# A long-convolution layer and two dense layers in one kernel: the filter's first layer on two 64-row tiles, signal factors in one transfer, one weight rounding a unit later

## The chip, the cores and the metric

The kernel runs on one core of a Trainium2 chip. The metric is the device time of one execution in microseconds (us), as the median of three runs. One further execution was taken with the profiler; its trace is what is read below.

## The reference

Three steps follow each other on 12480 positions (S) of 128 channels (D). The first is a causal convolution of length S with a filter that a small network makes from 64 position features; the filter is damped by a window exp(-0.01 pos). The other two are dense layers of width 2048 with different gates.

```python
h_filt = (np.maximum(pos_emb @ w1, 0.0) @ w2) * np.exp(-0.01 * pos)[:, None]     # (S, 128); w1 is 64x64
u = x * v
y = np.fft.irfft(np.fft.rfft(u, n=2*S, axis=1) * np.fft.rfft(h_filt, n=2*S, axis=0)[None], n=2*S, axis=1)[:, :S]
a = x * y
h = a @ w_in;   a = (h * np.clip(h + 3, 0, 6) / 6) @ w_out                        # 128 -> 2048 -> 128
h = a @ w_in2;  a = np.where(h > 0, h, np.exp(np.minimum(h, 0)) - 1) @ w_out2
```

## The kernel before

**The convolution as matmuls.** Position p is written as 128·row + column, with 98 rows (`H1`) and 128 columns (`N2`). Every sequence is folded first: columns 64+i and 63-i are added and subtracted, so that there are 64 pairs i (`HN`) with two halves. The transforms along rows and columns are then matmuls with tables of cosines and sines (`t1`, `rows`, `gm`, `cs`, `ti`).

**The start, which the change touches.**

- Six matmuls on zeros (L184, the pool `warm`) come first on TensorE.
- The position features lie in HBM already folded and transposed: `posT` has the 64 features of one column of a pair on partitions 0 to 63 and those of the other on 64 to 127, and for each pair i a block of `H1` columns. SyncE loads it in eight pieces (L239), pieces 0 to 7 of 4, 6, 7, 8, 9, 10, 10, 10 pairs.
- `filter_hidden` (L345) runs over the 64 pairs in ten groups, `HIDDEN`: 4, 4, six times 8, 4, 4. For each pair one matmul (L349) multiplies 98 rows by a block-diagonal `w1` of 128 columns, so both halves come out of one pass over all 128 partitions. Each group has its own PSUM buffer `pr`, four of which exist.
- ScalarE takes the ReLU of the second half of each pair, scaled by `RATIO[i]`, into `au` (L357). VectorE then makes sum and difference with the ReLU of the first half (L370), 256 elements at a time, in one sweep for every four pairs; in the last two groups VectorE also takes over part of ScalarE's work (L363). The result is `Rf` (read as `Rp` here), in `qb`.
- `signal(n)` (L333) makes u = x·v for four channels (L338) and folds it (L340, L341). There are 32 such signals. For n = 0 and 1 it runs on GpSimd, from n = 2 on VectorE; each loads its x and v by two transfers (L315, L316) six signals ahead.
- `first` (L391) is the first transform: 8 matmuls of 180 columns, two halves onto different output partitions, and copies by ScalarE (L399). `first_u(n)` needs `signal(n)`; `first_r(c)` needs all of `Rf`. The order on TensorE is the layer, `first_u(0)`, `first_u(1)`, `first_r(0)`, `first_r(1)`, then two signals and one filter chunk in turn, 48 in all.

All order is written by hand: each engine runs its instructions in the order of the code, and all loads of this part stand in SyncE's queue. Eight transfers at most are under way on that queue: a ninth waits until the first has landed.

Later stages follow on TensorE: `second_r`, `second_h`, `second_u` (L448, L457, L467), the column transforms (L495, L531) and the inverse (L654).

**The dense layers.** A unit is a tile of 512 positions by 256 of the 2048 columns. On TensorE unit n has `mm1` (L841, into `h`) and, four units later, `mm2` (L885, into `o`). Between them ScalarE takes the activation (`act1`, L851), VectorE the gate (L862), ScalarE rounds the result to its upper part (`hi`, L870, into `gs`) and VectorE subtracts for the lower part (`lo`, L875). Weights are split in the same manner, in 16 quarters `w{i}_{q}` (matrix i, quarter q): loaded (L709), rounded on ScalarE (L781), and the lower half made on GpSimd in two pieces (L788). The table `pieces` says in which unit each of the two pieces of a quarter is made; the rounding comes one unit before the first. Each piece on GpSimd also waits for the newest instruction on VectorE in the program's order (`last_dve`).

Of the kernel before, what the change touches and what calls it, by code (L numbers as in the profile page):

```python
# [15 lines left out]
ALU = mybir.AluOpType  # L16
# [10 lines left out]
HN = N2 // 2  # L27
NM = HN + 1
SP = H1 * N2
HP = H1 * HN  # L30
HD = D // 2
SHIFT = H1 // 4
TT = 512
# [34 lines left out]
def tables():  # L68
    n1, k1, k2 = np.arange(H1), np.arange(NK), np.arange(N2)
    i, m, a = np.arange(HN), np.arange(NM), np.arange(H1) - 2 * SHIFT - 1  # L70
    w = 2 * np.pi * (np.outer(n1 - SHIFT, k1) % N1) / N1
    c, s = np.cos(w), np.sin(w)

    t1 = np.stack([np.stack([c, -s], axis=2), np.stack([-s, -c], axis=2)], axis=1)
    k = k1[:, None] + N1 * k2
    w = np.pi * (((2 * i + 1)[:, None, None] * k) % (2 * L)) / L
    gm = np.concatenate([np.cos(w), np.sin(w)], axis=0)

    w = 2 * np.pi * (np.outer(k2, m) % N2) / N2
# [45 lines left out]
    ratio = np.tile(np.repeat(RATIO, 2), (H1, 1))  # L125
    return [np.ascontiguousarray(z, dtype=np.float32) for z in (t1, gm, cs, ti, rows, column, ratio)]


def folded(z):

    z = np.pad(z, ((0, SP - S), (0, 0))).reshape(H1, N2, -1)
    return np.stack([z[:, HN:], z[:, HN - 1::-1]], axis=1).transpose(0, 3, 1, 2)


@with_exitstack
def tile_kernel(ctx, tc, xc, vc, xT, posT, w1_d, w2_d, moe_w, t1_d, gm_d, cs_d, ti_d, rows_d, column_d, ratio_d, outT):
    nc = tc.nc
    w_dram = [nc.dram_tensor(f"w_scratch{i}", (128, FF), F32, kind="Internal").ap() for i in range(4)]

# [82 lines left out]
    xts, vts, uts = uvs[:DEEP], uvs[DEEP:2 * DEEP], uvs[2 * DEEP:]  # L222
# [8 lines left out]
    Rf = qb[:H1, RW:RW + RF].rearrange("p (g s i t) -> p s i g t", s=2, i=HN, t=2)
    Rp = qb[:H1, RW:RW + RF].rearrange("p (g s x) -> p s g x", s=2, x=2 * HN)
    w1s = qb[:, HP:HP + 2 * FO]
    ratio = qb[:H1, HP + 2 * FO:HP + 2 * FO + N2]
    GI = 4
    nc.scalar.dma_start(w1s, w1_d)
    edges = [0, 4, 10, 17, 25, 34, 44, 54, 64]
    for a, b in zip(edges, edges[1:]):
        nc.sync.dma_start(pos_t[:, a * H1:b * H1], posT[:, a * H1:b * H1])  # L239
    tab = const.tile([128, 8 * NK], F32, name="tab")  # L240
    t1, rows = (tab[:H1, i * 4 * NK:(i + 1) * 4 * NK].rearrange("p (f k) -> p f k", f=2) for i in range(2))
# [103 lines left out]
    def filter_hidden(i0, n):  # L345
        pr = bank("pr", [128, 2, 2, FO // 2, GI, 2])
        t = au[:H1, i0 * FO:(i0 + n) * FO].rearrange("p (b g j t) -> p b g j t", g=FO // 2, j=GI, t=2)
# [5 lines left out]
        def relu(b):  # L353
            i = i0 + b * GI
            own = GI if i < HN - 2 * GI else 2
            for j in range(own):
                nc.scalar.activation(t[:, b, :, j], pr[:H1, b, 1, :, j], AF.Relu, scale=float(RATIO[i + j]))  # L357
            return own

        def folds(b, own):  # L360
            i = i0 + b * GI
            if own < GI:
                nc.vector.scalar_tensor_tensor(  # L363
                    t[:, b, :, own:].rearrange("p g j t -> p g (j t)"),
                    pr[:H1, b, 1, :, own:].rearrange("p g j t -> p g (j t)"), 0.0,
                    ratio[:, 2 * (i + own):2 * (i + GI)].unsqueeze(1).to_broadcast([H1, FO // 2, 2 * (GI - own)]),
                    op0=ALU.max, op1=ALU.mult,
                )
            for x, op in enumerate((ALU.add, ALU.subtract)):
                nc.vector.scalar_tensor_tensor(  # L370
                    Rp[:, x, :, 2 * i:2 * (i + GI)], pr[:H1, b, 0].rearrange("p g j t -> p g (j t)"), 0.0,
                    t[:, b].rearrange("p g j t -> p g (j t)"), op0=ALU.max, op1=op,
                )

        owns = [relu(b) for b in range(n // GI)]
        for b, own in enumerate(owns):
            folds(b, own)

    for n in range(DEEP):
        load_signal(n)  # L380
        if n == 0:
            nc.sync.dma_start(ratio, ratio_d)
            nc.sync.dma_start(t1.rearrange("p f k -> p (f k)"), t1_d)
        if n == 1:
            nc.sync.dma_start(rows.rearrange("p f k -> p (f k)"), rows_d)
            nc.sync.dma_start(column, column_d)
# [337 lines left out]
    for i, banks in enumerate(BATCHES):  # L724
# [243 lines left out]
```

## Time and profile before

| | |
|---|---|
| median of 3 runs | 1324.15 us (1323.83 to 1326.51) |
| profiled execution | 1326.66 us |
| its span, first to last instruction | 1324.8 us |
| TensorE busy | 1314.0 us, 99% of the span |
| VectorE busy | 1134.2 us, 86% |
| ScalarE busy | 1005.8 us, 76% |
| GpSimd busy | 411.0 us, 31% |

The span is the time between the program's first and last instruction; 1.9 us of the profiled execution lie around it. A busy engine is not one at its peak: matmuls overlap in the pipeline, and their rate has to be read from how many start in a stretch. In the rows PE is TensorE, PEld its weight loads, DVE VectorE, ACT ScalarE, POOL GpSimd and SP SyncE.

### The profile page before, as it was taken

The numbers are of one execution on the slowest core, as the hardware profiler recorded it, in microseconds if no ns is written. First come the engines' busy times: TensorE is split into PE (matmuls) and PEld (weight loads), VectorE is DVE, ScalarE is ACT, GpSimd is POOL, SyncE is SP. The second block draws the span as 40 slices with busy tenths as digits, with TensorE's granted clock in tenths as the row PEclk, the third lists the DMA queues.
The fourth block names the chain that finished last, engine by engine and source line by source line (L and its number), as shares of the span: only waits on it lengthen the run. The fifth ranks groups of instructions, "written<-read, shape, count | busy, mean of one in ns | idle before, by whom it ended". The sixth has DMA issues, their size and how long they took to land.

```text
span 1324.8 us, 23014 instructions
## 1 busy us (share of the span) xinstructions
PE 1314.0 (99%) x9184; PEld 1128.0 (85%) x9184; DVE 1134.2 (86%) x1209; ACT 1005.8 (76%) x1210; POOL 411.0 (31%) x319
## 2 busy tenths in 40 slices
PE   9999999999999999999999999999999999999998
PEld 9999998788888888888888888888888888888898
DVE  6769876699988888888888888888888888888897
ACT  5677663398878887788877887888778878887776
POOL 1027741334233322222223323222222223322223
PEclk9999999999999999999999999999999999999999
DMA  8945338610000000000000000000000000000000
GB/s 270 249 141 161 111 97 260 197 54 19 9 9 1 9 8 8 1 9 9 9 9 0 8 9 8 0 9 8 8 1 9 8 8 1 8 8 9 8 7 14
DMA packets 33676, 58.80 MB, mean 44 GB/s; under 512 B 3962, under 2 KB 10272, under 8 KB 33568
## 3 DMA queue, kind: packets, MB, share of 16 engines
q1 hardware_dynamic: 27232, 50.18, 12.5%
q10 hardware_dynamic: 6336, 7.15, 1.7%
q8 instruction: 72, 1.18, 0.4%
q14 instruction: 36, 0.29, 0.1%
HBM read 46.73 MB, written 10.58 MB: 43 GB/s over the span
## 4 chain that ended last, share of the span: by engine, by line
PE 96%; DVE 1%; ACT 1%; issue 1%; DMA 0%; POOL 0%; ACTq 0%; SPq 0%; POOLq 0%
PE o L885 39%; PE h L841 39%; PE pa L395 4%; PE y L654 3%; PE z L467 3%; PE q L495 2%; PE r L448 1%; PE h L457 1%; PE pr L349 1%; PE q L531 1%; DVE gs L875 0%; DMA w<-w_scratch 0%; DVE g L864 0%; ACT gs L870 0%; ACT qb L460 0%
## 5 line engine op out<-in xcount | busy, mean ns | idle before, releaser
L885 PE MATMUL o<-gs,w 128*128 128x512 f32 (+1 forms) x2400 | 566.2, 384 | 1.2 <-DVE gs L875 1.1
L885 PEld LDWEIGHTS o<-gs,w 128*128 128x128 f32 x2400 | 445.1, 188 | 87.4 <-DVE gs L875 1.7
L854 POOL TENSOR_SCALAR a<-a 128x1024 f32<-128x1024 f32 (+1 forms) x200 | 295.3, 1477 | 707.2 <-ACT a L853 705.9
L875 DVE TENSOR_TENSOR gs<-g,gs 128x1024 fp32r<-128x1024 f32 (+1 forms) x400 | 481.3, 1203 | 6.8 <-ACT gs L870 6.0
L870 ACT CAST gs<-g 128x1024 fp32r<-128x1024 f32 (+1 forms) x400 | 409.9, 1025 | 52.8 <-DVE g L862 51.4
L862 DVE SCALAR_TENSOR_TENSOR g<-a,h 128x1024 f32<-128x1024 f32 (+1 forms) x200 | 238.8, 1194 | 117.5 <-ACT a L851 117.2
L841 PE MATMUL h<-x,w 128*128 128x512 f32 (+1 forms) x1200 | 298.1, 384 | 0.2 <-DVE g L864 0.2
L841 PE MATMUL h<-xs,w 128*128 128x512 f32 (+1 forms) x1200 | 297.9, 384 | 0.0
L853 ACT ACTIVATE a<-h 128x1024 f32<-128x1024 f32 (+1 forms) x200 | 201.2, 1006 | 89.7 <-PE h L841 88.5
L841 PEld LDWEIGHTS h<-xs,w 128*128 128x128 f32 x1200 | 223.1, 188 | 44.6 <-DVE g L862 0.4
L841 PEld LDWEIGHTS h<-x,w 128*128 128x128 f32 x1200 | 223.0, 188 | 43.8 <-ACT gs L870 0.5
L851 ACT ACTIVATE a<-h,bounds 128x1024 f32<-128x1024 f32 (+1 forms) x200 | 218.9, 1094 | 49.7 <-PE h L841 49.5
L864 DVE SCALAR_TENSOR_TENSOR g<-a,h 128x1024 f32<-128x1024 f32 (+1 forms) x200 | 237.5, 1188 | 0.2 <-POOL a L854 0.2
L289 POOL TENSOR_TENSOR cv<-cv 128x256 int32<-128x256 int32 x32 | 23.4, 730 | 126.1 <-DVE cv L286 120.3
L395 PE MATMUL pa<-tab,qb 98*64 98x180 f32 x512 | 41.6, 316 | 0.1
L395 PEld LDWEIGHTS pa<-tab,qb 98*64 98x64 f32 x512 | 37.7, 138 | 2.7 <-ACT qb L399 0.4
L788 POOL TENSOR_TENSOR w<-w 128x256 fp32r<-128x256 f32 x26 | 19.2, 741 | 40.0 <-DVE gs L875 19.4
L271 ACT ACTIVATE cv<-cv 128x256 int32<-128x256 uint32 x32 | 14.2, 444 | 21.4 <-DMA cv<-in_mw 9.6
L654 PE MATMUL y<-qb 128*64 128x98 f32 (+3 forms) x688 | 25.5, 249 | 2.8 <-issue 2.8
L486 POOL TENSOR_TENSOR qb<-qb,bp 128x1024 f32<-128x1024 f32 (+1 forms) x12 | 27.0, 2247 | 3.9 <-DVE bp L481 3.9
L817 ACT COPY y<-o 128x512 f32<-128x512 f32 (+1 forms) x25 | 14.4, 578 | 17.5 <-PE o L885 17.5
L654 PEld LDWEIGHTS y<-qb 128*64 128x64 f32 (+1 forms) x688 | 23.1, 137 | 4.9 <-issue 3.6
(98 smaller groups left out, 880.4 us busy)
## 6 DMA issues: line engine op xcount, KB each, us to landing
uv<-in_xc SPq DMA_DIRECT2D x32, 196.0 KB
out_T<-y SPq DMA_DIRECT2D x23, 256.0 KB
qb<-in_gm SPq DMA_DIRECT2D x22, 256.0 KB
cv<-in_mw SPq DMA_DIRECT2D x21, 256.0 KB
au<-in_xT SPq DMA_DIRECT2D x16, 268.0 KB
w_scratch<-cv ACTq DMA_DIRECT2D x32, 128.0 KB
w<-w_scratch SPq DMA_DIRECT2D x16, 256.0 KB
cv<-in_vc SPq DMA_DIRECT2D x20, 196.0 KB
```

The lines of the kernel that those rows point to most:

```text
L395: nc.tensor.matmul(pa[f * HN:(f + 1) * HN, j, :2 * NK], lhsT=src(j, f), rhs=table[:, f], start=True, stop=True)
L467: nc.tensor.matmul(z[:, j], lhsT=gm_of(k0 + j), rhs=spectrum(hf, k0 + j, 1)[:, :, 0], start=True, stop=True)
L654: nc.tensor.matmul(y[c * HD:(c + 1) * HD, b, off:off + w], lhsT=lhsT, rhs=rhs[:, H1 - w:], start=(b, c) in fresh, stop=done, skip_group_ch ...
L841: nc.tensor.matmul(h[:, j], lhsT=wslice(2 * m - 2, a, 2 * u + j), rhs=x[:, b], start=i == 0, stop=i == 2)
L851: paced[0] = nc.scalar.activation(a, h, AF.Relu, bias=three)
L853: nc.scalar.activation(a, h, AF.Exp)
L854: nc.gpsimd.tensor_scalar(a, a, 1.0, 0.0, op0=ALU.min, op1=ALU.max)
L862: last_dve[0] = nc.vector.scalar_tensor_tensor(g, a, 6.0, h, op0=ALU.min, op1=ALU.mult)
L864: last_dve[0] = nc.vector.scalar_tensor_tensor(g, a, -1.0, h, op0=ALU.add, op1=ALU.max)
L870: nc.scalar.copy(t[:, 0], g)
L875: last_dve[0] = nc.vector.tensor_tensor(out=t[:, 1], in0=g, in1=t[:, 0].bitcast(F32), op=ALU.subtract)
L885: nc.tensor.matmul(o[:, :WID[t]], lhsT=wslice(2 * m - 1, a, 2 * u + j), rhs=gs[:, b, j], start=u == 0 and j == 0 and i == 0, stop=u == NU ...
```

## The change

- The window is zero from position 10398 (`ZERO`) on, so the filter has only 82 rows (`HR`) that count; the layer, its folds, `posT` and the table `rows` are cut to 82 rows.
- The layer's matmul per pair becomes two, each over 64 partitions and 64 columns of `w1`, written into the two PSUM banks of `pr`.
- The folds run over the whole group, 512 elements for 8 pairs, and VectorE no longer takes over ReLU work; the table `ratio` and its load are gone.
- x and v of a signal come in one transfer of 4 KB for each partition. The table `t1` comes before the first signal. Signals 0 and 2 run on GpSimd, 1 and 3 on VectorE.
- In the dense layers the two lower pieces of quarter `w0_3` are made in units 3 and 4 and not 2 and 3, so its rounding moves from unit 1 to unit 2.

```diff
+HR = -(-ZERO // N2)
-HP = H1 * HN
+HP = HR * HN
...
+    xvs = [
+        z[:H1, i * 2 * VT:(i + 1) * 2 * VT].rearrange("p (t d f i) -> p t d f i", t=2, f=2, i=HN)
+        for z, i in ((uv, 0), (uv, 1), (cv, 0), (cv, 1), (uv, 2), (uv, 3))
+    ]
...
-            c = slice(n * DC, (n + 1) * DC)
-            nc.sync.dma_start(xts[n % DEEP], xc[:, c])
-            nc.sync.dma_start(vts[n % DEEP], vc[:, c])
+            nc.sync.dma_start(xvs[n % DEEP], xv[:, n])
...
-    EARLY, LOOK = 2, 4
+    EARLY, LOOK = (0, 2), 4
...
-        e = nc.gpsimd if n < EARLY else nc.vector
+        e = nc.gpsimd if n in EARLY else nc.vector
...
     def filter_hidden(i0, n):
-        pr = bank("pr", [128, 2, 2, FO // 2, GI, 2])
+        pr = bank("pr", [128, 2, FO // 2, 8, 2])[:HR, :, :, :n]
...
         for j in range(n):
-            nc.tensor.matmul(
-                pr[:H1, j // GI, :, :, j % GI], lhsT=pos_t[:, (i0 + j) * H1:(i0 + j + 1) * H1],
-                rhs=w1s.rearrange("p (s g t) -> p s g t", s=2, t=2), start=True, stop=True,
-            )
...
+            for r in range(2):
+                p = slice(r * FO, (r + 1) * FO)
+                nc.tensor.matmul(
+                    pr[:, r, :, j], lhsT=pos_t[p, (i0 + j) * HR:(i0 + j + 1) * HR],
+                    rhs=w1s[p].rearrange("p (g t) -> p g t", t=2), start=True, stop=True,
+                )
+        for j in range(n):
+            nc.scalar.activation(t[:, :, j], pr[:, 1, :, j], AF.Relu, scale=float(RATIO[i0 + j]))
+        a, b = (z.rearrange("p g j t -> p g (j t)") for z in (pr[:, 0], t))
+        for x, op in enumerate((ALU.add, ALU.subtract)):
+            nc.vector.scalar_tensor_tensor(Rp[:, x, :, 2 * i0:2 * (i0 + n)], a, 0.0, b, op0=ALU.max, op1=op)
...
+    load_table(0)
+    load_signal(0)
+    load_signal(1)
+    load_table(1)
+    nc.sync.dma_start(column, column_d)
+    for n in range(2, DEEP):
         load_signal(n)
...
-        (1, 0): (1, 1), (0, 3): (2, 3), (1, 1): (4, 5), (1, 2): (6, 7), (1, 3): (8, 9), (2, 0): (10, 11),
+        (1, 0): (1, 1), (0, 3): (3, 4), (1, 1): (4, 5), (1, 2): (6, 7), (1, 3): (8, 9), (2, 0): (10, 11),
...
-        "xc": folded(x),
-        "vc": folded(v),
+        "xv": np.stack([folded(z).reshape(H1, D // 4, 4, 2, HN) for z in (x, v)], axis=2),
...
-        "posT": folded(inputs["pos_emb"]).transpose(2, 1, 3, 0).reshape(2 * FO, HP),
-        "w1": w1,
+        "posT": folded(inputs["pos_emb"], HR).transpose(2, 1, 3, 0).reshape(2 * FO, HP),
+        "w1": np.tile(inputs["w1"], (2, 1)),
```

On VectorE the program begins with two memsets; these rows stand behind them. Before:

```order
L370 SCALAR_TENSOR_TENSOR qb<-pr,au 98x32x8 x28
L363 SCALAR_TENSOR_TENSOR au<-pr,qb 98x32x4
L370 SCALAR_TENSOR_TENSOR qb<-pr,au 98x32x8 x2
L363 SCALAR_TENSOR_TENSOR au<-pr,qb 98x32x4
L370 SCALAR_TENSOR_TENSOR qb<-pr,au 98x32x8 x2
L338 TENSOR_TENSOR uv<-uv,cv 98x512
L340 TENSOR_TENSOR qb<-uv 98x4x64
L341 TENSOR_TENSOR qb<-uv 98x4x64
```

The same place on VectorE in the changed kernel:

```order
L357 SCALAR_TENSOR_TENSOR qb<-pr,au 82x32x8 x4
L357 SCALAR_TENSOR_TENSOR qb<-pr,au 82x32x16 x12
L357 SCALAR_TENSOR_TENSOR qb<-pr,au 82x32x8 x4
L336 TENSOR_TENSOR uv<-uv 98x512
L338 TENSOR_TENSOR cv<-uv 98x4x64
L339 TENSOR_TENSOR cv<-uv 98x4x64
```

32 folds and two ReLU pieces have become 20 folds, and the first signal behind them is number 1, which `first_u(1)` waits for; before it was number 2.

On SyncE this is the beginning of the queue of loads. Before:

```order
L239 DMA qb<-in_posT 128x392
L239 DMA qb<-in_posT 128x588
L239 DMA qb<-in_posT 128x686
L239 DMA qb<-in_posT 128x784
L239 DMA qb<-in_posT 128x882
L239 DMA qb<-in_posT 128x980 x3
L315 DMA uv<-in_xc 98x512
L316 DMA uv<-in_vc 98x512
L382 DMA qb<-in_ratio 98x128
L383 DMA tab<-in_t 98x360
L315 DMA uv<-in_xc 98x512
L316 DMA uv<-in_vc 98x512
```

The same place in the changed kernel:

```order
L360 DMA qb<-in_posT 128x328
L360 DMA qb<-in_posT 128x492
L360 DMA qb<-in_posT 128x574
L360 DMA qb<-in_posT 128x656
L360 DMA qb<-in_posT 128x738
L360 DMA qb<-in_posT 128x820 x3
L363 DMA tab<-in_t 98x360
L314 DMA uv<-in_xv 98x1024 x2
L363 DMA tab<-in_rows 98x360
L372 DMA column<-in_column 128x3
```

The pieces of `posT` stand first in both and are smaller; `ratio` is gone, and `t1` stands ahead of the first signal.

On ScalarE this is the start of the dense layers. The rounded weights are `w_0_...` for `w1_0`, `w_3_...` for `w0_3` and `w_1_...` for `w1_1`; `a<-h` is `act1`, `gs<-g` is `hi`. Before:

```order
L851 ACTIVATE a<-h,bounds 128x1024 x2
L781 CAST w_0_3439<-w_0_3439 128x512
L781 CAST w_3_3441<-w_3_3441 128x512
L870 CAST gs<-g 128x1024
L851 ACTIVATE a<-h,bounds 128x1024
L870 CAST gs<-g 128x1024
L851 ACTIVATE a<-h,bounds 128x1024
L870 CAST gs<-g 128x1024
L781 CAST w_1_3443<-w_1_3443 128x512
```

The same place in the changed kernel:

```order
L839 ACTIVATE a<-h,bounds 128x1024 x2
L769 CAST w_0_3460<-w_0_3460 128x512
L858 CAST gs<-g 128x1024
L839 ACTIVATE a<-h,bounds 128x1024
L858 CAST gs<-g 128x1024
L769 CAST w_3_3462<-w_3_3462 128x512
L839 ACTIVATE a<-h,bounds 128x1024
L858 CAST gs<-g 128x1024
L769 CAST w_1_3464<-w_1_3464 128x512
```

The rounding of `w0_3` has moved behind the `hi` of units 0 and 1. GpSimd's pieces keep their order.

## Rows read from the trace of the kernel before

**Rows 1.** The page: span, and the chain that ended last by engine.

```profile
span 1324.8 us, 23014 instructions
...
PE 96%; DVE 1%; ACT 1%; issue 1%; DMA 0%; POOL 0%; ACTq 0%; SPq 0%; POOLq 0%
```

**Rows 2.** Chain that ended last, 0 to 300 us: start, length, what.

```profile
3.98 15.59 PE pr L349 x128
19.57 2.64 PE pa L395 x32
...
22.23 56.47 PE pa L395 x735
78.70 3.77 PE r L448 x32
...
84.29 2.04 PE h L457 x32
...
188.77 22.55 PE q L495 x736
```

**Rows 3.** The layer's matmuls in two stretches: duration ns min/median/max, first and last start.

```profile
L349 PE MATMUL pr<-qb x14: 421/421/502, 3.8 to 6.6; 128*98 128x128 f32 x14
L349 PE MATMUL pr<-qb x114: 272/273/374, 6.9 to 19.3; 128*98 128x128 f32 x114
```

**Rows 4.** Timeline, 5 to 24 us: start, length, instruction, [idle before it <-released by].

```profile
6.93 0.32 SPq L382 DMA_DIRECT2D qb<-in_ratio  x1
...
9.13 1.02 ACT L357 ACTIVATE au<-pr 98x64 f32<-98x64 f32 x8 [1.18 <-PE pr L349]
...
13.09 0.36 SPq L386 DMA_DIRECT2D column<-in_column  x1
...
14.66 1.28 POOL L338 TENSOR_TENSOR uv<-uv 98x512 f32<-98x512 f32 x1 [13.49 <-DMA uv<-in_vc]
15.43 1.42 DVE L370 SCALAR_TENSOR_TENSOR qb<-pr,au 98x256 f32<-98x256 f32 x4 [0.33 <-ACT au L357]
...
17.39 1.29 POOL L338 TENSOR_TENSOR uv<-uv 98x512 f32<-98x512 f32 x1
...
22.22 0.68 DVE L338 TENSOR_TENSOR uv<-uv,cv 98x512 f32<-98x512 f32 x1
...
22.94 0.43 DVE L340 TENSOR_TENSOR qb<-uv 98x256 f32<-98x256 f32 x1
23.28 0.42 DVE L341 TENSOR_TENSOR qb<-uv 98x256 f32<-98x256 f32 x1
```

**Rows 5.** Timeline, VectorE on 1024 elements, one behind the other.

```profile
90.52 1.22 DVE L481 TENSOR_TENSOR qb<-z,qb 128x1024 f32<-128x1024 f32 x1
...
91.65 1.24 DVE L481 TENSOR_TENSOR au<-z,qb 128x1024 f32<-128x1024 f32 x1
```

**Rows 6.** Timeline, start of the dense layers.

```profile
259.72 0.61 ACT L781 CAST w<-w 128x512 fp32r<-128x512 f32 x1
...
261.30 0.62 ACT L781 CAST w<-w 128x512 fp32r<-128x512 f32 x1 [0.97 <-DMA w<-w_scratch]
261.83 1.04 ACT L870 CAST gs<-g 128x1024 fp32r<-128x1024 f32 x1
...
264.18 1.43 PE L885 MATMUL o<-gs,w 128*128 128x512 f32 x5 [0.74 <-DVE gs L875]
...
267.44 1.22 DVE L875 TENSOR_TENSOR gs<-g,gs 128x1024 fp32r<-128x1024 f32 x1
...
268.79 0.74 POOL L788 TENSOR_TENSOR w<-w 128x256 fp32r<-128x256 f32 x1 [1.58 <-ACT a L851]
...
269.59 1.67 PE L885 MATMUL o<-gs,w 128*128 128x512 f32 x6
```

**Rows 7.** Busy PE, PEld, DVE, ACT, POOL in stretches; granted clock; DMA share; GB/s.

```profile
7.00:22.00 15.00, 15.00 (x147) 14.56 (x145) 11.05 (x33) 8.11 (x58) 5.36 (x6) 1.00 0.95 309
...
40.00:60.00 20.00, 20.00 (x266) 18.80 (x264) 14.81 (x33) 13.93 (x28) 0.00 (x0) 1.00 0.95 244
```

More of the change, by code (lines that the diff above doesn't have):

```diff
@@ L124, in tables, with folded, tile_kernel @@
     column = np.stack([np.tile(np.exp(-0.01 * (HN + i)), 2), sign, -sign], axis=1)
[L125 to L131, printed above, removed]
+    return [np.ascontiguousarray(z, dtype=np.float32) for z in (t1, gm, cs, ti, rows, column)]
+def folded(z, n=H1):
+    z = np.pad(z, ((0, SP - S), (0, 0))).reshape(H1, N2, -1)[:n]
     return np.stack([z[:, HN:], z[:, HN - 1::-1]], axis=1).transpose(0, 3, 1, 2)
 @with_exitstack
-def tile_kernel(ctx, tc, xc, vc, xT, posT, w1_d, w2_d, moe_w, t1_d, gm_d, cs_d, ti_d, rows_d, column_d, ratio_d, outT):
+def tile_kernel(ctx, tc, xv, xT, posT, w1_d, w2_d, moe_w, t1_d, gm_d, cs_d, ti_d, rows_d, column_d, outT):
     nc = tc.nc
@@ L221, in tile_kernel @@
     DEEP = 6
-    xts, vts, uts = uvs[:DEEP], uvs[DEEP:2 * DEEP], uvs[2 * DEEP:]
+    xvs = [
+        z[:H1, i * 2 * VT:(i + 1) * 2 * VT].rearrange("p (t d f i) -> p t d f i", t=2, f=2, i=HN)
+        for z, i in ((uv, 0), (uv, 1), (cv, 0), (cv, 1), (uv, 2), (uv, 3))
+    ]
+    uts = uvs[2 * DEEP:]
     rest = qb[:, RW:AR0]
@@ L230, in tile_kernel @@
     pos_t = qb[:, :HP]
[L231 to L235, printed above, removed]
+    Rf = qb[:HR, RW:RW + RF].rearrange("p (g s i t) -> p s i g t", s=2, i=HN, t=2)
+    Rp = qb[:HR, RW:RW + RF].rearrange("p (g s x) -> p s g x", s=2, x=2 * HN)
+    w1s = qb[:, HP:HP + FO]
     nc.scalar.dma_start(w1s, w1_d)
-    edges = [0, 4, 10, 17, 25, 34, 44, 54, 64]
-    for a, b in zip(edges, edges[1:]):
-        nc.sync.dma_start(pos_t[:, a * H1:b * H1], posT[:, a * H1:b * H1])
     tab = const.tile([128, 8 * NK], F32, name="tab")
-    t1, rows = (tab[:H1, i * 4 * NK:(i + 1) * 4 * NK].rearrange("p (f k) -> p f k", f=2) for i in range(2))
+    tabs = [tab[:H1, i * 4 * NK:(i + 1) * 4 * NK] for i in range(2)]
+    t1, rows = (z.rearrange("p (f k) -> p f k", f=2) for z in (tabs[0], tabs[1][:HR]))
     qss = [z[:, :4 * N2] for z in (tab, qb[:, OWN:], qb[:, OWN + 4 * N2:])]
@@ L335, in signal @@
             load_signal(n + DEEP - 1)
-        e = nc.gpsimd if n < EARLY else nc.vector
-        xt = xts[n % DEEP]
-        e.tensor_tensor(out=xt, in0=xt, in1=vts[n % DEEP], op=ALU.mult)
+        e = nc.gpsimd if n in EARLY else nc.vector
+        xt, vt = (xvs[n % DEEP][:, i] for i in range(2))
+        e.tensor_tensor(out=xt, in0=xt, in1=vt, op=ALU.mult)
         ut = uts[n % len(uts)]
@@ L345, in filter_hidden @@
     def filter_hidden(i0, n):
-        pr = bank("pr", [128, 2, 2, FO // 2, GI, 2])
-        t = au[:H1, i0 * FO:(i0 + n) * FO].rearrange("p (b g j t) -> p b g j t", g=FO // 2, j=GI, t=2)
+        pr = bank("pr", [128, 2, FO // 2, 8, 2])[:HR, :, :, :n]
+        t = au[:HR, i0 * FO:(i0 + n) * FO].rearrange("p (g j t) -> p g j t", j=n, t=2)
         for j in range(n):
-            nc.tensor.matmul(
-                pr[:H1, j // GI, :, :, j % GI], lhsT=pos_t[:, (i0 + j) * H1:(i0 + j + 1) * H1],
-                rhs=w1s.rearrange("p (s g t) -> p s g t", s=2, t=2), start=True, stop=True,
-            )
@@ L353, in relu @@
[L353 to L367, printed above, removed]
-                )
[L369 to L379, printed above, removed]
-        load_signal(n)
[L381 to L386, printed above, removed]
+            for r in range(2):
[3 more added lines that the diff above has]
+                    rhs=w1s[p].rearrange("p (g t) -> p g t", t=2), start=True, stop=True,
+                )
@@ new lines, in filter_hidden, with load_pos, load_table @@
+        for j in range(n):
[3 more added lines that the diff above has]
+            nc.vector.scalar_tensor_tensor(Rp[:, x, :, 2 * i0:2 * (i0 + n)], a, 0.0, b, op0=ALU.max, op1=op)
+    def load_pos(a, b):
+        nc.sync.dma_start(pos_t[:, a * HR:b * HR], posT[:, a * HR:b * HR])
+    def load_table(i):
+        nc.sync.dma_start(tabs[i], (t1_d, rows_d)[i])
@@ L387, in tile_kernel @@
+    edges = [0, 4, 10, 17, 25, 34, 44, 54, 64]
+    for a, b in zip(edges, edges[1:]):
+        load_pos(a, b)
+    load_table(0)
[4 more added lines that the diff above has]
+    for n in range(2, DEEP):
+        load_signal(n)
     for i0, n in HIDDEN:
@@ L928 @@
     weights = [inputs["moe_w_in"], w_out[0], inputs["moe2_w_in"], w_out[1]]
-    t1, gm, cs, ti, rows, column, ratio = tables()
-    w1 = np.zeros((2 * FO, 2 * FO), np.float32)
-    for i in range(2):
-        w1[i * FO:(i + 1) * FO, i * FO:(i + 1) * FO] = inputs["w1"]
+    t1, gm, cs, ti, rows, column = tables()
     arrays = {
-        "xc": folded(x),
-        "vc": folded(v),
+        "xv": np.stack([folded(z).reshape(H1, D // 4, 4, 2, HN) for z in (x, v)], axis=2),
         "xT": x[ORDER].T,
-        "posT": folded(inputs["pos_emb"]).transpose(2, 1, 3, 0).reshape(2 * FO, HP),
-        "w1": w1,
+        "posT": folded(inputs["pos_emb"], HR).transpose(2, 1, 3, 0).reshape(2 * FO, HP),
+        "w1": np.tile(inputs["w1"], (2, 1)),
         "w2": np.tile(inputs["w2"], (2, 1)),
@@ L945 @@
         "column": column,
-        "ratio": ratio,
     }
@@ L956 @@
     out = nc.dram_tensor("out_T", (D, S), F32, kind="ExternalOutput").ap()
-    names = ("xc", "vc", "xT", "posT", "w1", "w2", "t1", "gm", "cs", "ti", "rows", "column", "ratio")
+    names = ("xv", "xT", "posT", "w1", "w2", "t1", "gm", "cs", "ti", "rows", "column")
     g = {k: aps[f"in_{k}"] for k in names}
@@ L960 @@
         tile_kernel(
-            tc, g["xc"], g["vc"], g["xT"], g["posT"], g["w1"], g["w2"], [aps[f"in_mw{i}"] for i in range(4)],
-            g["t1"], g["gm"], g["cs"], g["ti"], g["rows"], g["column"], g["ratio"], out,
+            tc, g["xv"], g["xT"], g["posT"], g["w1"], g["w2"], [aps[f"in_mw{i}"] for i in range(4)],
+            g["t1"], g["gm"], g["cs"], g["ti"], g["rows"], g["column"], out,
         )
```

## Prediction

> **What bounds the kernel now.** I read the page first: of the chain of work that ended last, 96% is TensorE and 1% each VectorE and ScalarE [rows 1]. So only what makes TensorE start or finish something earlier counts. Then the chain in order of time, for the two places that the change touches. At the start it runs through the layer (3.98 to 19.57 us), two signal firsts (to 22.21), and from 22.23 without a gap through the other 46 firsts to 78.70 [rows 2]. The mark that I follow is therefore the start of `first_r(0)`, 22.23 us; all behind it stands back to back on TensorE for 56 us and should move with it.
>
> Within the layer the clock matters. The first 14 passes (an fp32 matmul is two passes here) last 421 ns and start 0.22 us apart (14 from 3.8 to 6.9); the other 114 last 272 ns and start 0.11 us apart (6.9 to 19.3) [rows 3]. [...] TensorE is the pacer of the layer: ScalarE (1.02 us for eight ReLUs) and VectorE (1.42 us for four folds) both wait in each group [rows 4]. The loads are ahead: SyncE can issue `ratio` only when piece 2 of `posT` has landed (6.93) and `column` when piece 7 has (13.09) [rows 4], which TensorE uses from about 17.
>
> At the start of the dense layers ScalarE's second rounding, of `w0_3`, waits 0.97 us for its transfer and holds up `hi` of unit 0, until 261.83; TensorE's first `mm2` then waits for the lower part, until 264.18, 0.74 us idle [rows 6].
>
> **The layer in the changed kernel.** A pair costs four passes of 64 columns on half the partitions each. The nearest row is `second_h`: 64-row tiles in turn, 128 columns, 32 passes in 2.04 us, 64 ns each; `second_r` with full tiles takes 3.77 us for 32, 118 ns [rows 2]. So two row tiles run at a time. For 64 columns half of 64 is 32 ns, and the column tiles of L495 with 64 columns give 22.55/736 = 31 ns [rows 2]; but 82 columns of weights are loaded for each 64 that stream, and if the load sets the pace of `second_h` it is 64·82/128 = 41 ns. I take 35, near the two rows of like size, with 31 and 41 as ends. [...]
>
> [...]
>
> Now in steps. TensorE starts the layer at 3.79 as before (behind the warm-up). At 4·65 ns for a pair 12 pairs are done at 6.9, four more at 140 ns by 7.5, so the third group (pairs 8 to 15) ends near 7.6. Piece 2 is 0.84 times as large (82/98 rows) and ahead of 6.9, so at most a few tenths are waited for it. ScalarE's eight ReLUs take until 8.8. From there VectorE is the pacer: four folds of 256 take 1.42 us, the first three 0.33 each [rows 4]; two of 1024 start 1.13 apart [rows 5]; a straight line gives 0.60 for 512. Twelve of these and four of 256 are 7.2 + 1.35 = 8.55 us: the folds end at about 17.4 (22.31 before). TensorE needs 8·0.14 = 1.12 and ScalarE some 1.15 us for a group against VectorE's 1.20, so they keep up. The ends: 0.67 (two of 256, nothing gained by width) adds 12·0.07 = 0.8; 41 ns makes TensorE's group 1.31 and adds 0.7; both together no more than 1.2, since they stand side by side.
>
> The stall then goes to a new place: `signal(1)`, before on GpSimd, is queued behind the folds on VectorE. It takes 0.72 + 0.34 + 0.42 = 1.48 us by the rows of `signal(2)` [rows 4], so its second half is there at 18.9, `first_u(1)` runs until 20.1 (56.47/46 = 1.23 each), and `first_r(0)` starts at 20.1. `first_u(0)` doesn't bind: of `posT` 2.69 MB are loaded instead of 3.21, ahead of signal 0 stand 0.14 MB of `t1` more, so x and v have landed with 0.38 MB less ahead, 1.2 us earlier at 309 GB/s [rows 7], 13.4; GpSimd needs 17.39 − 14.66 = 2.73 us [rows 4] and is done at 16.2; TensorE waits for that and ends it at 17.4. TensorE thus idles some 2 us in two pieces between the layer's end (about 14.5) and 18.9.
>
> So `first_r(0)` starts 22.23 − 20.1 = **2.1 us earlier** (1.3 to 2.5). At nothing I cost: signal 2 on GpSimd, done near 19 and first needed at 22.6; signal 3 on VectorE, done near 20.4 and needed at 23.8; the single transfers, since from 22 us on TensorE waits for none of them; `t1` and `rows`, landed before 15. If that cover went, each would cost its own lateness, at most about 1 us.
>
> **The rounding a unit later.** `hi` of unit 0 can follow the first rounding, at 260.3 and not 261.83 [rows 6]: its input is ready. Then `lo(0)` ends near 262.6, just when TensorE finishes its fifth `mm1`, and `mm2` of unit 0 runs on without a stall: 1.4 us earlier than before. Part is given back. The second lower piece of `w0_3` now stands on GpSimd right ahead of the first of `w1_1`, both behind `lo(2)`. Before, the one piece ran at 268.79, behind `lo(2)` at 267.44, and released `mm2` of unit 2 at 269.59 [rows 6]. Now `lo(2)` is 1.45 earlier, at 266.0, its end at 267.25; two pieces of 0.72 end at 268.8 and `mm2` of unit 2 starts there, while TensorE is ready at 268.05. Net **0.75 us**; from there on a unit takes 2.72 us on TensorE either way. The ends are 0.3 (the moved rounding also delays `act1` of unit 3 by its 0.6) and 1.4 (no waiting on GpSimd).
>
> **The sum.** 2.1 + 0.75 = 2.85 us (1.6 to 3.9). The profiled execution would go from 1326.66 to 1323.8, its span from 1324.8 to 1322.0. That execution stands 2.5 above the median of the runs shown, so of the median: 1324.15 − 2.85 = **1321.3**. This is 0.215%, and 0.2% (2.65 us) is about what a measurement of this kernel can tell from no change.
>
> **Rivals.**
>
> - *The clock rises later.* Before, TensorE was at work without a pause from 1.05 to 7 us when the step came. The new layer can pause for pieces of `posT`, and half its passes use half the rows. If the step came two groups later, the pairs in between take 0.26 instead of 0.14 us: 12·0.12 = 1.4 us, of which VectorE's queue hides little. 1322.7. [...]
> - *The gain is lost before 79 us.* DMA is busy 0.95 of 40 to 60 us [rows 7]. If transfers there were the pace, an earlier start would not matter, and only the rounding's part would stay: 1323.4. Against it: TensorE is busy all 20 us, the new kernel moves 0.57 MB less, and in larger rows.
> - *Row tiles don't overlap in this shape, and loads set the pace* (the other side). A pass then costs 118·82/128 = 75 ns (`second_r`'s rate, by columns loaded) and twice that before 7 us: 22 passes until 7, the other 234 take 17.6 us, the layer ends at 24.6, the last folds near 26, `signal(1)` at 27.5, `first_r(0)` at 28.7: 6.5 later, less 0.75, 1329.9. With the pace by streamed columns, 59 ns, the layer ends at 20.4, the folds near 21.7 and `first_r(0)` starts at 24.4: 1325.6. It decides from the point where the folds end after 20.3 us. [...] Against it `second_h`, whose tiles alternate in the same way.
>
> **Chances.** The forecast 0.70 (its own range 1320.2 to 1322.5), the clock 0.13, the gain lost 0.10, no overlap 0.07. To leave out no more than 2 in 10, the range reaches from 1319.6 (both upper ends, and some tenths for the scatter of the median) to 1323.8. Faster by over 0.2% means under 1321.5, a bit over the forecast's middle: three quarters of its 0.70, so 0.53. Within 0.2%: the rest of it, the clock and the lost gain, 0.41. Slower 0.06: most of the third rival.
>
> **What would show it.** Right: the layer's passes pairwise at 35 ns, folds of 512 at 0.60 without waiting from 8.8 on, their end near 17.4, `signal(1)` straight behind, `first_r(0)` near 20.1, no idle TensorE from there to 76.6; at the dense layers `hi` of unit 0 right behind one rounding, and a stall of some 0.7 before `mm2` of unit 2, released by GpSimd. Wrong: passes of 421 ns or the like beyond 8 us, folds that wait for ScalarE, signal 0 landing after 16, or `first_r(0)` early but the start of `second_r` still at 78.7.

## The result: slower by 9 us

The changed kernel takes 1333.86 us in the median of 4 runs (1331.71 to 1335.87), the kernel before beside it 1324.78 (1323.83 to 1326.51): 9.1 us more. The ratio on record is 1.0056, with a 95% interval of [1.0039, 1.0073], which is 5 to 10 us. The forecast was 1321.3, its range ended at 1323.8. The profiled execution took 1335.87 us, 9.21 more than that of the kernel before, and it is these two that the account below compares. The mean granted clock of TensorE is 0.994 to 0.996 in all four executions; in the profile of the kernel before it is 1.000.

The page of the changed kernel, span and chain by engine (before: [rows 1]):

```profile
span 1334.1 us, 23189 instructions
...
PE 93%; issue 2%; DVE 2%; ACT 1%; POOL 1%; ACTq 0%; POOLq 0%; DVEq 0%
```

Its chain, start, length, what (before: [rows 2]; the layer is L349, the firsts are L383, `second_r` is L436, the column transforms L483 and L519, the inverse L642):

```profile
3.98 9.00 PE pr L349 x208
12.97 2.08 issue
15.05 0.82 PE pr L349 x16
...
17.55 2.00 DVE qb L357 x5
19.55 1.33 DVE uv L336
...
20.90 0.84 DVE cv L338
...
21.88 63.86 PE pa L383 x747
85.75 3.77 PE r L436 x32
...
176.03 4.11 PE q L483 x124
...
215.27 0.44 issue
215.72 4.14 PE q L483 x127
219.85 1.26 issue
```

`second_r` starts at 85.75 where it was 78.70: 7.05 us later, and 9.2 later than the 76.6 that the forecast implies. Where the chain comes to the column transforms (176.03) the distance is 7.27, at the end of the last `y` it is 9.70, at the end of the program 9.3. So most of the loss is made before 86 us, and some 2.4 us more come between 176 and 265.

Three things stand in the first 34 us. In the midst of the layer TensorE stands still for 2.08 us and waits for nothing that the profile shows (`issue` in the chain). Then VectorE is late with `signal(1)`. And from 16.76 us TensorE's granted clock is 0.5. Windows of the changed kernel (columns as in [rows 7]):

```profile
8.14:12.19 4.05, 4.05 (x116) 4.05 (x115) 3.37 (x6) 3.57 (x30) 0.00 (x0) 1.00 0.98 308
...
14.00:17.00 3.00, 1.95 (x48) 1.91 (x47) 0.94 (x3) 1.11 (x11) 1.81 (x2) 0.96 0.93 264
17.00:24.00 7.00, 5.62 (x31) 3.35 (x30) 6.93 (x13) 1.65 (x10) 4.05 (x5) 0.50 0.79 202
24.00:33.00 9.00, 9.00 (x64) 7.11 (x62) 4.12 (x10) 3.00 (x5) 0.00 (x0) 0.50 0.77 218
33.00:40.00 7.00, 7.00 (x90) 6.31 (x88) 4.74 (x11) 4.38 (x10) 0.00 (x0) 0.94 0.61 170
```

The column before the last two is the granted clock as a share of full speed: 0.50 from 17 to 33 us, although TensorE is busy without a gap from 21.88 on. The record of the clock begins at 6.52 with 1.00, where the layer's passes go from 70 to some 35 ns apart; it has 0.50 from 16.76 and 1.00 again from 33.83.

Timeline of the changed kernel:

```profile
8.82 6.06 DVE L357 SCALAR_TENSOR_TENSOR qb<-pr,au 82x512 f32<-82x512 f32 x10 [0.99 <-ACT au L354]
...
15.05 2.10 PE L349 MATMUL pr<-qb 64*82 64x64 f32 x48 [2.08 <-issue]
...
17.23 3.35 PE L383 MATMUL pa<-tab,cv 98*64 98x180 f32 x16
...
19.06 1.26 POOL L336 TENSOR_TENSOR cv<-cv 98x512 f32<-98x512 f32 x1 [1.19 <-DMA cv<-in_xv]
19.47 1.40 DVE L336 TENSOR_TENSOR uv<-uv 98x512 f32<-98x512 f32 x1
20.40 1.05 POOL L338 TENSOR_TENSOR qb<-cv 98x256 f32<-98x256 f32 x1
...
20.90 0.83 DVE L338 TENSOR_TENSOR cv<-uv 98x256 f32<-98x256 f32 x1
...
22.52 0.68 DVE L336 TENSOR_TENSOR cv<-cv 98x512 f32<-98x512 f32 x1
```

### The profile page after: what moved, and what is told of

Read it like the earlier page. It is cut to its first block, busy times and chain, and to the rows that moved or that the text cites. A ratio compares the mean times of both kernels' runs of the same rounds, so it can differ in the third digit from the quotient of the medians.

```text
span 1334.1 us, 23189 instructions
## 1 busy us (share of the span) xinstructions
PE 1318.4 (99%) x9312; PEld 1127.3 (85%) x9312; DVE 1135.9 (85%) x1195; ACT 1006.2 (75%) x1214; POOL 411.9 (31%) x319
## 4 chain that ended last, share of the span: by engine, by line
PE 93%; issue 2%; DVE 2%; ACT 1%; POOL 1%; ACTq 0%; POOLq 0%; DVEq 0%
PE h L829 38%; PE o L873 38%; PE pa L383 5%; PE y L642 3%; PE z L455 2%; PE q L483 2%; PE r L436 1%; PE h L445 1%; PE q L519 1%; PE pr L349 1%; DVE qb L469 0%; POOL a L842 0%; ACT gs L858 0%; DVE gs L863 0%; DVE au L469 0%
## 5 line engine op out<-in xcount | busy, mean ns | idle before, releaser
L383 PE MATMUL pa<-tab,qb 82*64 82x180 f32 (+1 forms) x512 | 47.4, 338 | 0.0
L383 PEld LDWEIGHTS pa<-tab,qb 82*64 82x64 f32 (+1 forms) x512 | 41.2, 149 | 4.7
L383 PE MATMUL pa<-tab,cv 98*64 98x180 f32 x256 | 27.1, 341 | 1.4 <-DVE cv L338 1.3
L642 PE MATMUL y<-qb 128*64 128x98 f32 (+3 forms) x688 | 25.9, 250 | 2.5 <-issue 2.5
```

What stands on the lines that cost most here:

```text
L383: nc.tensor.matmul(pa[f * HN:(f + 1) * HN, j, :2 * NK], lhsT=src(j, f), rhs=table[:, f], start=True, stop=True)
L642: nc.tensor.matmul(y[c * HD:(c + 1) * HD, b, off:off + w], lhsT=lhsT, rhs=rhs[:, H1 - w:], start=(b, c) in fresh, stop=done, skip_group_ch ...
```

## What the 2.08 us are

Up to the stop 220 passes are done: 12 of the warm-up and 208 of the layer's 256. That is behind 52 pairs, where no piece of `posT` begins (44 and 54 are the nearest), and the last piece had landed by 12.38, where SyncE issues the load that waits for it. What moves at that time is a transfer of another kind. DMA of the changed kernel, from 12.15 to 13.45 us (packets, MB, share):

```profile
q1 hardware_dynamic: 85, 0.30, 80.8%
q8 instruction: 1, 0.02, 5.9%
```

This one packet has 16384 bytes and runs from 12.19 to 13.42; TensorE goes on 1.64 us behind its end. Over the whole program the queue moved 73 such packets, and TensorE's 18624 recorded weight loads and matmuls (one of each is a pass) make 255 for each packet. So a packet is a block of some 256 instructions, or about 127 passes with a few semaphore waits, and TensorE had run out of them. Counted back by 256 recorded instructions, pass 94 came at 8.14 us; if the next block is asked for there, it began 4.05 us later, with DMA busy 0.98 (first window above). The mark is rough: one packet in the kernel before began 0.7 us ahead of its own. There the mark came at 14.16 and the packet at 16.46; as the next block lasted until 25.46, nobody waited. The stops of later stages are of the same kind. Of what the profile records for TensorE (weight loads, matmuls and semaphore waits) 449 entries stand ahead of the stop in the layer; the eight stops of 0.28 to 1.26 us without a releaser between 200 and 265 us, among them those at 215.27 and 219.85 in the chain above, all stand whole multiples of 256 entries behind it.

The theory: **the row tiles double the passes of a pair at half the time each, TensorE uses up its instructions three times as quickly, and the next block stands behind the loads of `posT` and x/v; this pause, and the one ahead of `first_u(1)`, take the clock back.** So far the first half rests on counts, the second is a guess. Rival A: half-row passes lower the clock by themselves. Rival B: the stop is a late load.

## The experiments

Each ratio is to the kernel before in the same comparison, with its 95% interval. e1 to e4 ran on one chip, e5 to e8 and e12 on another, e9 to e11 on a third, so how often the clock fell is compared across these with care. The mean clock of an execution says how much it fell, but not where; where it fell is read from the one profiled execution of each run.

**e1_mixed.** Fewer instructions: 28 pairs on whole tiles (with folds of 256), the rest on row tiles.

```diff
+WHOLE = (24, 32, 40, 56)
...
+        if whole:
...
+                nc.tensor.matmul(
+                    pr[:, j // 4, :, :, j % 4], lhsT=pos_t[:, (i0 + j) * HR:(i0 + j + 1) * HR],
+                    rhs=w1s.rearrange("p (s g t) -> p s g t", s=2, t=2), start=True, stop=True,
+                )
```

> The changed kernel, but 28 of the 64 pairs (groups 24, 32, 40 and 56) go through one matmul on all 128 partitions again, the other 36 on two 64-row tiles; the layer then has 400 recorded instructions on TensorE and not 512. Theory (TensorE runs out of instructions behind its 449th recorded one, and the pause makes the clock fall): no stop inside the layer, which ends near 16.6; folds end near 18.4, first_r(0) starts near 21, granted clock 1.00 from 7 us on, time 1322 to 1324. Rival A (half-row passes by themselves let the clock fall): the clock falls near 17 us as in the changed kernel, time near 1330. Rival B (the stop is a late piece of posT): a stop of about 2 us stays near 13 to 15.

1.0058 [1.0039, 1.0077], 1334.31 us where the theory had 1322 to 1324. The stop is gone, as the theory has it, but the clock falls at 22.87, after TensorE has waited 2.63 us for `signal(1)`. Timeline and windows:

```profile
21.29 0.49 PE L403 MATMUL pa<-tab,cv 98*64 98x180 f32 x2 [2.63 <-DVE cv L339]
```

```profile
19.00:23.00 4.00, 1.43 (x14) 1.09 (x16) 3.93 (x6) 0.53 (x2) 2.64 (x3) 0.98 0.77 230
23.00:33.00 10.00, 10.00 (x70) 8.12 (x68) 5.18 (x12) 3.39 (x6) 0.00 (x0) 0.50 0.70 206
```

I had counted only the first pause; the second is enough.

**e2_whole.** All pairs on whole tiles (`WHOLE = tuple(range(0, HN, 4))`).

> The changed kernel with the matmul of the layer as before (one per pair on 128 partitions, 256 recorded instructions) and all else changed. Theory: TensorE paces the layer until 19.3, the folds end near 20.6, signal(1) on VectorE near 22.1, first_r(0) starts near 23.4, 1.2 later than before; clock 1.00; with 0.6 back at the dense layers 1325 to 1326. If the loss came from the single transfers or from signal(1) on VectorE and not from the tiles, it would be near 1330 here too.

1.0059 [1.0037, 1.0080], and not the 1.001 of the theory. There is no stop and no half-row pass in this kernel, and the clock falls at 23.54, behind a wait of 1.91 us for `signal(1)`:

```profile
19.00:23.00 4.00, 2.09 (x25) 1.50 (x25) 3.97 (x11) 1.40 (x6) 1.52 (x3) 1.00 0.87 229
23.00:33.00 10.00, 10.00 (x75) 9.91 (x72) 5.52 (x13) 3.39 (x6) 0.00 (x0) 0.53 0.64 208
```

So row tiles are not needed for the fall, against rival A; for this case the expectation named the single transfers or `signal(1)` on VectorE, and e12 tells these two apart. One of its five executions kept a mean clock of 0.999 and took 1330.47; the others, at 0.995 to 0.997, took 1334.58 to 1338.81.

**e3_whole_late.** e2 with two pieces of `posT` behind the signals.

```diff
+    for a, b in spans[:6]:
+        load_pos(a, b)
     load_table(0)
     load_signal(0)
     load_signal(1)
     load_table(1)
     nc.sync.dma_start(column, column_d)
+    for a, b in spans[6:]:
+        load_pos(a, b)
```

> As e2_whole, with the last two pieces of posT loaded behind t1, signals 0 and 1, rows and column, so that TensorE stands still for about 2 us at pair 44 without a single half-row pass. Theory (the pause lets the clock fall): the granted clock is 0.50 for 10 us or more soon behind the pause, and the time is 1331 to 1336. Rival A (half-row passes): clock 1.00 throughout, only the pause is lost, 1327 to 1328.

1.0072 [1.0055, 1.0090]. The profiled execution has pauses of 0.95 and 1.91 us, keeps its clock and takes 1328.82; the three others have a mean clock of 0.996 and take 1335.42 to 1339.70. The pause that I made was half as long as meant, and one profile can't say which of the two mattered.

**e4_count.** 32 more recorded instructions ahead of the layer.

```diff
+    for i in range(8):
+        nc.tensor.matmul(warm[i % 4][:, :8], lhsT=zeros, rhs=zeros[:, :8], start=True, stop=True)
```

> The changed kernel with 8 tiny matmuls on zeros (8 columns, 32 recorded instructions) behind the warm-up. Theory (a block of instructions is used up): the stop comes 32 recorded instructions earlier in the layer, behind pair 48 and not behind pair 52, again behind the 449th. Rival B (a late transfer of posT or of a signal): the stop stays behind pair 52. Time as the changed kernel, 1332 to 1336.

Chain, and the window up to the stop:

```profile
3.98 3.21 PE warm L186 x16
7.20 9.69 PE pr L351 x192
16.89 0.75 issue
17.64 1.40 PE pr L351 x32
```

```profile
0.00:17.30 17.30, 15.84 (x220) 15.74 (x221) 5.77 (x13) 6.80 (x45) 3.35 (x11) 1.00 0.85 258
```

12 + 16 + 192 = 220 passes again, four pairs earlier in the layer. Rival B is out: the place goes by instructions, not by data. The stop is shorter because the block has more time: the tiny passes take 3.21 us, and the clock rises only at 12.43 (6.52 in the changed kernel), so that 192 passes of the layer take 9.69 us. From there it stayed at 1.00, in spite of the stop and of a pause of 2.35 us ahead of `first_u(1)` (21.57 to 23.92); the time of this one execution, 1330.61, was below what I expected for that reason.

**e5_mixed_early.** e1 with `signal(1)` ahead of the last folds.

```diff
     for i0, n in HIDDEN:
+        if i0 == HN - 8:
+            us = [signal(0), signal(1)]
         filter_hidden(i0, n)
-    us = [signal(n) for n in range(LOOK)]
+    us += [signal(n) for n in range(2, LOOK)]
```

> e1_mixed (no stop for instructions in the layer) with signal(1) on VectorE ahead of the folds of the last two groups and not behind them. Theory (a pause of TensorE of about 2 us in this stretch lets the clock fall, whatever its cause): signal(1) starts near 17.6, first_u(1) follows first_u(0) within 0.3 us, first_r(0) starts near 20.5, granted clock 1.00 from the rise to the end, 2 to 3 us faster than before (ratio about 0.998). Rival A (half-row passes or something else in the new start let the clock fall): the clock falls as in e1_mixed, slower than before by 5 us or more.

1.0022 [1.0008, 1.0036]. The mean clock is 0.999 or 1.000 in 9 of 12 executions (e1: 0.996 or less in all 6), and these take 1327.55 to 1330.45, the three at 0.996 1332.10 to 1334.93. That far the theory holds. But nothing is won: pauses of 0.35 us for `posT`, 0.47 and 0.82 for `signal(1)` remain, and `second_r` starts at 78.5 as before.

**e6_fill.** e1 with work on zeros in the pause.

```diff
             first_u(us.pop(0), n)
+            if n == 0:
+                fill = [bank("fill", [128, N2]) for _ in range(2)]
+                for i in range(10):
+                    nc.tensor.matmul(fill[i % 2], lhsT=zeros, rhs=zeros, start=True, stop=True)
```

> e1_mixed with ten matmuls on zeros (20 passes, some 2.4 us) on TensorE between first_u(0) and first_u(1), where it waited 2.63 us for signal(1); the data come no earlier. Theory: the granted clock stays at 1.00, first_r(0) starts near 22.9, the time is that of before within 2 us, 7 us or more below e1_mixed. Rival A: the clock falls as in e1_mixed and the time is the same as there, ratio about 1.006.

1.0034 [1.0019, 1.0049]; no execution at 0.996 or less, against all six of e1 (on another chip). In the trace the clock at the start stays:

```profile
23.00:33.00 10.00, 10.00 (x136) 9.46 (x134) 8.83 (x21) 6.36 (x12) 0.00 (x0) 1.00 0.85 236
```

The same firsts now do 136 passes in 10 us, where e1 did 70. This is the cleanest of the runs: the data came no earlier, only TensorE did not stand still. The time is 4.5 us above before all the same, more than expected: 1.4 us at `second_r`, the rest in later stops, one of which (2.24 us at 235) brings 3.4 us of half clock of its own.

**e7_before_pause.** The kernel before with `EARLY` 1 and not 2.

> The kernel before with one number changed: signal 1 runs on VectorE behind the folds and not on GpSimd. No row tiles, no new transfers. TensorE then waits some 2.5 us between first_u(0) and first_u(1). Theory: the granted clock falls to 0.50 behind this pause for 10 us or more in most executions, ratio 1.005 to 1.008. Rival A (row tiles): the clock stays at 1.00, only the pause is lost, ratio about 1.002.

1.0031 [1.0018, 1.0044]. A pause of 2.58 us, yet the clock stays at 1.00 in the profile:

```profile
22.70 1.53 PE L395 MATMUL pa<-tab,cv 98*64 98x180 f32 x15 [2.58 <-DVE cv L340]
```

and the mean clock is 0.997 in one of ten executions, 0.998 to 1.000 in the others. Here the theory misses: a pause of that length does not take the clock every time, and the outcome is nearer to what was expected of rival A. Against rival A e2 still stands, which has no row tiles either and whose clock fell; what makes e2 and e7 differ was not found. Of the 0.3% in time the profile shows the pause, by which `second_r` starts 1.8 us later; short falls in the other executions would fit their mean clocks, but aren't shown.

**e8_after_early.** The changed kernel with the edit of e5: only the stop is left.

> The changed kernel, all 64 pairs on row tiles, with signal(1) ahead of the folds of the last two groups. The stop of about 2 us behind the 449th recorded instruction stays, the second pause goes. Theory: the stop alone lets the clock fall in most executions, ratio 1.002 to 1.005; first_r(0) near 22.5 if it doesn't fall before. If only the pause ahead of first_u(1) mattered: clock 1.00 and ratio 1.000 or less.

1.0040 [1.0020, 1.0060]; 4 of 5 executions at 0.994 to 0.996, the fifth, at 1.000, takes 1328.59. Chain and window:

```profile
3.98 8.46 PE pr L349 x208
12.44 2.49 issue
14.93 3.15 PE pr L349 x46
```

```profile
15.00:19.00 4.00, 4.00 (x56) 3.70 (x57) 2.07 (x3) 2.14 (x16) 2.81 (x4) 0.56 0.91 264
```

So the stop alone is enough for a fall, too: half clock from 15.48 to 22.30. But `second_r` starts only 0.6 us later than in the kernel before. Of the 6.0 us by which the profiled execution is longer, 5.8 come between 166 and 262 us, where TensorE stands still for longer and the clock falls once more, from 233.93 to 237.34, behind a stop of 1.38 us.

**e9_pieces.** The kernel before with `(0, 3): (3, 4)` alone.

> The kernel before with only the rounding of w0_3 a unit later. The prediction's term: 0.75 us, which the median can barely show (ratio 0.9994); in the trace the time from the last y to the dense layers in full swing falls from 98.9 to about 98.2. Rival: the profiled wait of 0.97 us for the transfer of w0_3 was that execution's own, and the term is near nothing. The trace also shows once more how long the kernel before stands still between 205 and 255 us for blocks of instructions (5.4 us in the first profile): if this is scatter, it differs by a microsecond or more here.

1.0010 [0.9994, 1.0026]: no gain that can be measured. It is weighed below.

**e10_mixed_pool.** e1 with `EARLY` (0, 1).

> e1_mixed with signal(1) on GpSimd behind signal(0), as in the kernel before, and signals 2 and 3 on VectorE. Theory: pauses of TensorE at the start of 0.6 us at most, first_r(0) starts near 20.7, second_r near 77.1 (1.5 before the kernel before), clock 1.00; the time is the kernel before's less 1 to 2 us if the waits for instruction blocks between 205 and 255 us stay as they are, ratio 0.998 to 1.001. Rival (the changed start costs those later waits some 2 us in every case, as e5_mixed_early had it): ratio 1.001 to 1.002 in spite of the earlier second_r.

1.0033 [1.0018, 1.0048]. Another miss: `second_r` starts at 80.2 and not 77.1. TensorE now pauses 0.77 us for `posT` at 7.6 and four more times, 0.17 to 0.61 us, for the signals, the first of which GpSimd could begin at 16.1 and not at 14.4 as in e1, since its load came later; mean clock 0.994 to 0.997 in 5 of 12.

**e11_thin.** The changed kernel with fewer loads under way.

```diff
     for i0, n in HIDDEN:
-        filter_hidden(i0, n)
+        relu = filter_hidden(i0, n)
+        if i0 == 8:
+            t1_load = load_table(0)
+            tc.add_manual_dep(t1_load.ins, relu.ins.name, ...)
+            load_signal(0)
...
```

> The changed kernel with t1, all signals, rows and column issued only once ScalarE has done the third group (near 8.8), so that three and not eight transfers stand ahead when TensorE passes its 193rd recorded instruction near 8.1. Theory (the block of instructions waits behind the data transfers under way): it starts 2 to 3 us after that mark and not 4.06, and the stop behind the 449th shrinks from 2.1 to under 1 us. Rival (the block's delay is fixed): 4 us and a stop of 2 us as before.

Pass 94 comes at 9.60, the packet at 9.95, 0.35 us later and not 4.05, and the layer runs through. Window between the two marks, and chain:

```profile
9.60:9.95 0.35, 0.35 (x10) 0.35 (x8) 0.19 (x1) 0.13 (x2) 0.00 (x0) 1.00 0.57 206
```

```profile
3.98 12.61 PE pr L349 x256
...
17.18 2.00 DVE qb L357 x5
```

With DMA at 0.57 and not 0.98 the block is there at once, so its delay isn't fixed. In the profiles of five other kernels the packet begins 2.30 us behind the same mark (the kernel before, DMA 0.94), 3.25 (e4, 0.88), 3.41 (e12, 0.95), 4.05 (the changed kernel, 0.98) and 4.70 (e8, 1.01). That the other transfers hold it up fits e11 against the rest and is what the edit changed; among the five the delay doesn't follow the share closely, and e11 is one execution. The layer is no quicker for it: the clock rises only at 10.31 here (6.52 in the changed kernel), and the folds end at 19.18, 0.37 earlier. The clock falls here as well, from 20.55 to 34.20, beside a wait of 2.22 us for `signal(1)`, and once more from 252.66 to 259.48 behind a stop of 3.03 us (1339.85 us in its one execution).

**e12_rest.** e2 with `EARLY` (0, 1).

> The changed kernel without the row tiles (one matmul per pair, as before) and with signal(1) back on GpSimd; what stays is the 82 rows, the single transfers of x and v, t1 ahead of the first signal and the rounding a unit later. Theory (the row tiles with their stop for instructions and signal(1) on VectorE are the whole loss): TensorE paces the layer until about 19.2 and has no pause over 0.3 us up to first_r(0), the clock stays at 1.00 in nearly all executions, ratio 0.998 to 1.001. Rival (the single transfers or the order of the loads cost something too, at the start or in the later waits for instruction blocks): ratio 1.002 or more with the clock at 1.00.

0.9999 [0.9988, 1.0011], mean clock 1.000 in all 12 executions. Chain and window:

```profile
3.98 15.32 PE pr L352 x128
19.30 10.83 PE pa L403 x139
```

```profile
23.00:33.00 10.00, 10.00 (x134) 9.33 (x132) 9.27 (x22) 6.82 (x13) 0.00 (x0) 1.00 0.90 237
```

No pause from 3.98 until `second_r` starts, 0.5 us earlier than before. What e12 leaves out, the row tiles (with the wide folds that go with them) and `signal(1)` on VectorE, is the loss; the 82 rows, the single transfers, the order of loads and the rounding together cost and bring nothing that can be measured. From e2 it differs by `EARLY` alone, that is by which engine has signals 1 and 2: 1.0059 there, 0.9999 here. No run was measurably faster than the kernel before.

## Why the prediction was wrong

- *Passes at 35 ns: right.* 116 passes in 4.05 us are 34.9 ns (first window). Folds of 512 take 6.06/10 = 0.61 us, 0.60 was forecast. Row tiles overlap; the third rival is out. The 65 ns for a pass of the first 12 pairs was an estimate that no run shows; in its place the changed kernel has 38 passes 70 ns apart until its clock record begins at 6.52, and the 48th pass starts at 6.88, near the forecast 6.9.
- *"TensorE needs 8·0.14 = 1.12 [us for a group]": the step that failed first.* I took the supply of instructions for given. The folds ended at 19.55 and not at the forecast 17.4: 2.15 us, the length of the stop. After 220 passes (449 recorded instructions) TensorE had nothing left: the next block, the packet of 16384 bytes, came from 12.19 to 13.42, and TensorE stood from 12.97 to 15.05.
- *`signal(1)` in 1.48 us: too low.* Its rows were of VectorE alone. In the changed kernel GpSimd does `signal(2)` at the same time: 1.40 for the product and 0.83 for the first half, 2.23 together, against 0.68 + 0.43 = 1.11 [rows 4]; the next product, without GpSimd beside it, takes 0.68 again (22.52). In e4 GpSimd is done with `signal(2)` before, and the two take 0.68 and 0.43 once more. `first_u(1)` started at 21.88 for 18.9: 2.1 from the stop and 0.9 from here, although it needed only the first half of `signal(1)` and the forecast waited for the second.
- *Signal 0: later than forecast, without effect.* GpSimd began it at 15.11 and not at 13.4, and between 13.6 and 16.1 in the other runs with these transfers in this order, so the bytes ahead of a load didn't give its landing. `first_u(1)` was later still.
- *The idle TensorE was costed at nothing.* "TensorE thus idles some 2 us in two pieces" stands in the prediction as a remark. It cost the most: the 47 firsts from 21.88 on take 63.86 us, where 46 took 56.47 [rows 2], so 47 take 57.7: 6.2 us for the clock. With the 3.0 before, that is the 9.2 by which `second_r` missed the forecast. The first rival had the clock rise later, at 1.4 us; a fall had no price. In the profiles of the changed kernel, e1, e2 and e8 the clock fell behind a pause of 2.08, 2.63, 1.91 and 2.49 us; in the changed kernel the fall came 1.7 us after TensorE had gone on (15.05 and 16.76), and in the profiles of e3, e4 and e7 it did not come behind 1.91, 2.35 and 2.58 us.
- *The rounding: mechanism right, gain not there.* In the profiled execution the first pass of `mm2` that needs the lower part starts 7.3 us behind the last `y` and not 8.5 (1.2; 1.4 was forecast), `mm2` of unit 2 then waits 0.50 for GpSimd (0.7), and the stage gains 0.56 (0.75). But e7, which has the old order, does without the 0.97 us of [rows 6], because its `w0_3` was there in time (both roundings, one behind the other, in the row below), and needs 0.5 us less than the changed order from the last `y` to the steady units. The term rested on one execution's late transfer. In the profile of e9 the stretch is 0.55 us shorter than in that execution, as in the changed kernel; in time its interval holds both nothing and the forecast 0.75 us.

```profile
263.19 1.13 ACT L781 CAST w<-w 128x512 fp32r<-128x512 f32 x2
```

- *The 2.4 us between 176 and 265* were in no rival. Stops for instruction blocks in this stretch sum to 4.9 us in the changed kernel, 3.6 in the kernel before (in the profiled execution, 1326.66 us), 1.5 in e9 (1323.03) and 6.0 in e12 (1329.46), all at full clock and with the same code there. They differ more from profile to profile than the 1.3 us between the first two, so I take this part for scatter; it isn't shown. All idle time of TensorE from the column transforms to the last `y` is 2.4 to 5.5 us in the three profiles with the old loads and 4.6 to 9.0 in the eleven with the new ones; e12, with 7.5 in its profile, is as fast as the kernel before over twelve executions all the same. One profile of each run can't part scatter from cause here; that the shift of the block borders in e1, e5 and e10 (5.3 to 6.2 us of stops) adds to it is possible and was not tried apart.

What stays open: why the clock falls behind some pauses of 2 us and not behind others (1.91 us did it in e2; 1.91 in e3, 2.35 in e4 and 2.58 in e7 did not in the profiles). Shown is that without pauses it doesn't fall at the start (e12, none of 12), and that with a filled pause it stayed (e6). What a fall costs is read in the firsts: 6.2 us in the changed kernel. Executions of one kernel with and without a low mean clock lie 4 to 11 us apart (e2, e3, e8), but later stops have their share in that.

## What to carry to other kernels

Count instructions, not only their time: where passes get short, ask how many microseconds 256 instructions last (at 35 ns a pass 128 passes take 4.5), and what the DMA queues carry while the next block must come (here it began 0.35 us behind its mark in e11, 4.05 in the changed kernel). And price each pause that a faster stage opens on TensorE by the clock that it can cost in the stage behind it (6.2 us in the firsts of the changed kernel); a stage that is quicker but waits in pieces can be worse than one that paces without a gap (1333.86 us against 1324.78).

## What the runs showed of the hardware

- TensorE's instructions came in packets of 16384 bytes, 73 in the changed kernel and one for 255 recorded weight loads and matmuls, on a DMA queue of their own (q8). The start of the first lay 0.35 us behind the mark with DMA at 0.57 (e11) and 4.05 behind it with DMA at 0.98; where TensorE stood, it went on 1.43 to 1.64 us behind the packet's end (e8, e4, the changed kernel).
- Once fallen, the clock stayed at half while TensorE worked without a gap: 11.95 us of its 17.07 in the changed kernel (21.88 to 33.83), 10.24 in e2 (23.54 to 33.78), 6.82 in e8 (15.48 to 22.30).
- VectorE's SBUF products and sums took twice as long while GpSimd did the same kind of work (1.40 against 0.68 us); folds that read PSUM did not (four in 1.42 us beside `signal(0)` [rows 4], and four in 1.41 without GpSimd in e1).
